# DeltaNet and a low-rank mixer on one core: where the second unit of each batch's first pass is multiplied by its inverse

## The chip, the cores and the metric

The kernel runs on one core of a Trainium2 chip. The metric is device time in microseconds, lower is better. Three runs of the kernel before gave 590.03, 590.49 and 590.49 us, a median of 590.49.

## The reference

Two blocks follow each other. The first is a DeltaNet layer over 4 batches, 8 heads, 768 steps and 48 channels, a recurrence with a 48 x 48 state per head; the second is a mixer over the 768 tokens of 384 channels, with a rank-32 product over the tokens and a two-layer perceptron over the channels.

```python
k_n = k / (np.linalg.norm(k, axis=-1, keepdims=True) + 1e-06)
for t in range(S):
    y[:, :, t] = einsum('bhd,bhde->bhe', q[:, :, t], state)
    v_old = einsum('bhde,bhd->bhe', state, k_n[:, :, t])
    state += beta[:, :, t] * einsum('bhd,bhe->bhde', k_n[:, :, t], v[:, :, t] - v_old)
x = y.transpose(0, 2, 1, 3).reshape(B, S, H * D)          # (4, 768, 384)
u = x + (x.transpose(0, 2, 1) @ U @ V).transpose(0, 2, 1)  # U (768, 32), V (32, 768)
out = u + np.maximum(u @ w_ch1, 0.0) @ w_ch2               # 384 -> 1536 -> 384
```

The arrays of the mixer arrive in float64 and are turned into float32 on the chip.

## The kernel before

The recurrence is done in chunks of 64 steps. A batch has twelve chunks (c = 0 to 11) and is split into two units of six chunks each: unit n = 2 * batch + half, so units 0 and 1 are the first batch. For a unit the kernel forms, for all eight heads and six chunks together:

- the products of the keys with themselves and with the queries (`grams`: transposes L668 or L405 on PE, copies L682 on ACT, products L704, then L714 and L725 on ACT, L717 and L736 on DVE);
- the norms and the scales with beta (`norms`: the square root L611 on ACT, then L614 to L619 on DVE);
- the inverse Z of a triangular 64 x 64 matrix per chunk and head (`blocks`): a transpose L781, a substitution on DVE step by step (L790 and L796), a transpose back L803, and joins of the 32 x 32 blocks on PE and ACT (L847 to L926).

`recur` then walks over the chunks. With s the state, a chunk needs z = Z (v - K s) and gives s + K z (L1135 on PE, L1147 on DVE, tile `s`) and the output (L972 and L986 on PE, copied to X by L956 on ACT). There are two ways to z, chosen by the set `LATE` of unit numbers. For a unit that is not in LATE, `prepare` forms Z K (L1011 on PE, L1030 on ACT) and Z v (L1022, L1035) ahead, in two halves of three chunks, and a chunk takes one product (L1107) and one subtraction (L1120, tile `z`). For a unit in LATE the chunk takes the product with the plain keys (L1066), subtracts (L1078, tile `w`), multiplies by Z (L1090) and copies (L1099, tile `z`):

```python
nc.vector.tensor_tensor(out=w..., in0=vn[:, cu]..., in1=p_b, op=ALU.subtract)   # L1078
for j, par, g in heads:
    nc.tensor.matmul(states(p_z)[half(g ^ par), par, j], pg[half(g), par, cu, j],
                     w[half(g), 2 * par + j], start=True, stop=True)             # L1090
z = zs[c] = small.tile([128, 4, D], FP32, name="z", bufs=3)
nc.scalar.copy(z.rearrange("p (r j) d -> p r (j d)", r=2), p_z)                  # L1099
```

At the same time the mixer's weights are read in fourteen slices and turned from float64 bits into float32 by five DVE steps (L1244, L1250, L1256, L1262, L1272) and one ACT step (L1229) each; the slice `u_sb` is the first. Two buffers, `X` and `wide`, and for two slices `hs`, take the raw slices in turn, and DVE frees them with L1262.

When all twelve chunks of a batch stand in X, the mixer takes it in three groups of 256 tokens. `front` forms tt = U^T x once per batch (L1469 on PE, L1476 on DVE), the rank-32 product (L1486) and its sum into X (L1495 on DVE), and turns the group around (L1514, or L405 where it is done in quadrants of the PE array; the copy to `ut` is L1517 on ACT). `wide` does the two channel layers (L1580, L393 in quadrants, and L1545; then L1695 and L1620). Some groups of the later batches use sums of blocks that save products (L1430, L1412, L1607).

Nothing is ordered by a scheduler while it runs. Each part of the kernel is a Python generator, and a table `ORDER` (L147) holds, for every engine and for the DMA queues of SP, a written list of part numbers that says whose next instruction comes. `PARTED` (L264) names the parts that work in 64 x 64 quadrants of the PE array. Part 1 loads half of the first unit's keys from ACT's queue and then issues a warm-up square root on a constant tile (L559); part 8 is `norms` of unit 0, 9 and 19 are the key products of units 0 and 1, 11 and 21 their `blocks`, 2 the first half of beta's transposes (L579, L587), 4 the recurrence of batch 0, 78 the weights, 81 the first `front`. A change of the table that a square root or another function needs is put into the program as an instruction of its own.

Of the kernel before, what the change touches and what calls it, by code (L numbers as in the profile page):

```python
# [26 lines left out]
def kernel(  # L27
# [100 lines left out]
    def advance(i, value, at):  # L128
# [20 lines left out]
        9.0 9.1 9.0.0.0 9.1.0.0 2*2 19.0 19.1 3 19.0.0.0 3 19.1.0.0 10.0 10.1 10.0.0.0 20.0 11.4 10.1.0.0  # L149
        11.4 11.2*2 11.4*2 11.2*2 20.1 11.4*4 20.0.0.0 11.2*4 20.1.0.0 4.1 4.0*2 4.1 21.2*2 4 4.4 21.2 4  # L150
        21.2 4.5 4 21.4*2 21.2 4 4.5 4.6 4*2 21.2 4.6 21.2*2 4.7 4*2 4.8 4.7 4 21.4 4.9 4 21.4 4 4.9 4.8
        4.2*2 21.4*2 4 4.10 21.4*2 4*2 4.10 4.11 4*2 4.11 4.3 32.0 31.0 4.3 31.1 4.12 4 31.0.0.0 31.1.0.0 4
        4.12 32.1 4.13 4*2 4.13 4.14 4 4.15 4 4.14 4.15 79 32.0.0.0 81 32.1.0.0 81*2 40.0 82 98.0*2 39.0
        39.1 82 98.1 40.1 39.1.0.0 39.0.0.0 98.1 98.2 33.2*2 98.2 98.3*2 98.4 33.4*2 33.2 98.4 33.2 98.5
        33.4*2 33.2*2 98.5 98.7 83 33.2 33.4 33.2 33.4 98.7 33.4*2 98.8 5 5.0 5 40.1.0.0 5 98.8 5.1 5 98.9 5
        98.9 5 5.1 98.9 5 98.9 5.2 5 98.10 5 5.2 5.3 5 99.0 5 99.0 5 5.3 5.4 5 99.0 5 99.0 5.5 5 99.1*2 5
        5.4 99.1*2 5.5 40.0.0.0 5 83 99.2*2 99.3*2 99.4 48.0 99.4 41.2*2 47.0 99.7 47.1 47.0.0.0 47.1.0.0
        41.4*2 99.5*2 48.1 41.2 41.4*2 41.2 99.7 99.8 48.1.0.0 5 99.8 5.6 5 48.0.0.0 5 99.9 5 99.9 5.7 5*2
        99.9 5 5.6 99.9 5.8 5.7 5 99.10 5*2 100.0 5.9 5 100.0 5.8 5 100.0 5 100.0 5.9 5 5.10 5 100.1 5.11 5
        5.10 100.1 5 5.11 100.1*2 84 100.2*2 100.3*2 100.4*2 100.5 100.7 100.5 49.2*2 55.0.0.0 84 55.1.0.0  # L160
        100.7 100.8 49.2 49.4*2 49.2 100.8 84 100.9*2 6 85 100.9 6 100.9 56.0.0.0 56.1.0.0 6 100.10 49.4*2
        6.0 6 101.0*2 85 6.1 6 101.1*2 6 101.1 6 101.1 6.2 6 101.2*2 6.1 6 101.2*2 6 6.3 6.2 101.3 6 101.3 6
        6.4 6.3 6 101.4 6 101.4 6.5 6 101.4 6 101.4 6.4 6 6.5 101.5*2 101.7*2 57.2*2 57.4*2 86 57.4*2 57.2*2
        101.8*2 101.9*2 63.0.0.0 101.10 6 101.10 6 63.1.0.0 102.0*2 86 6.6 6 102.1*2 64.0.0.0 6 6.6 102.2 6
        102.2 6.7 6 102.2*2 6 6.7 102.3 6 102.3 6.8 6 102.3 6 102.3 6.9 6 102.4 6 102.4 6.8 6 102.4 6 102.4
        6.10 6 102.5*2 6.9 6.11 102.5 6 102.5 6.10 6 102.7 6.11 102.7 87 102.7*2 64.1.0.0 87 102.8*2 102.9*2
        102.10 71.0.0.0 103.0*2 71.1.0.0 103.1*2 103.2*2 103.3*2 65.4*2 65.2*2 103.4*2 72.1.0.0 65.2*2
        65.4*2 103.5*2 87 103.7 7 72.0.0.0 7 103.7 7 7.0 103.8*2 7.1 7 103.8*2 7 88 7 103.9*2 7 7.1 7.2 7
        103.10 7 7.2 104.0 7 104.0 7.3 7 104.0*2 7 7.3 7.4 104.1 7 104.1 7 104.1*2 7.5 7 7.4 104.2 7 104.2
        88 104.3*2 7 7.5 73.4*2 73.2*2 104.4*2 104.5 73.4*2 73.2*2 104.5 7 104.7 7 7.6 7 104.7 7 7.7 104.8  # L170
        7.6 7 104.8 7 104.8 7 104.8 7 7.7 7.8 7 104.9 7 7.8 7.9 7 104.9 7 89 7 104.10 7 7.9 7.10 7 7.11 7
        104.10 7 7.10 7.11 79 93.2 93.1 79 89 93.4 93.2 93.1 93.3 93.2 93.3 93.4 93.1 93.5 93.1 93.2 93.1
        94.2 94.3 93.1 90 94.3 94.4 94.2 90 94.1 105.3*2 94.1 94.2 90 94.1 94.5 94.1 94.4 94.2 105.4*2 105.5
        94.1 105.5 94.1 91 105.6 95.2 95.1 91 95.4 106.3 95.2 95.3 95.1 106.3 95.1 95.3 95.4 95.1 95.2
        106.4*2 95.5 95.1 106.5 95.2 96.3 95.1 106.5 96.1 106.6 92 96.4 96.2 96.1 92 96.2 96.4 96.1 96.2
        96.3 96.2 96.1 107.3*2 107.4*2 96.1 96.5 107.5*2 96.1 107.6 97.1 97.4 97.2 97.1 97.3 97.2 97.1
        108.3*2 97.1 97.3 97.2 97.5 108.4*2 97.1 97.2 108.5 97.1 108.5 108.6 97.4 109.3*2 109.4*2 109.5*2
        109.6
# [3 lines left out]
        78.14 3 10.0.0.0 11.2 18 78.15 21 78.15 10.1.0.0 10.0.0.0 21 18 21 11.4*2 10.1.0.0 11.4 21*3 11.2*3  # L182
        8 21 78.15 21*7 20.0.0.0*2 21*2 20.1.0.0 21 20.1.0.0 78.15*2 21.2 21.4 18 78.16 4 78.16*4 4 78.17*2
        4 21.2*3 78.17*3 4 78.18*2 4 78.18*3 4 78.19*2 4 78.19 4 78.19 4 78.19 78.20*2 4 78.20 21.4 4
        78.20*2 21.4 78.21 21.4 78.21*4 4 78.22*2 4 78.22*2 4 78.22 4 78.23*2 4 78.23*3 78.24*5 4 78.25*2
        31.0.0.0*2 31.1.0.0*2 4 33 4 30 4 78.25 4 33*2 4 78.25*2 33*2 78.26 32.0.0.0 78.26 81 33 78.26 81
        32.1.0.0*2 78.26 33 78.26 33 82 33*2 32.0.0.0 30 33*8 33.4 33.2 78.26.1*3 39.0.0.0 78.27 98.2.1*3
        39.1.0.0 78.26.1 39.0.0.0 30 78.27*4 39.1.0.0 33.2*3 33.4*2 78.27.1 33.4 41 98.5.1*2 78.27.1*2
        98.7.0 98.5.1 78.27.1 38 83 41 98.6 5 98.7.1 41*3 38 98.8.0 5 98.8.1 41*3 5 41 5 41*2 40.1.0.0
        98.9.0 41 98.9.1 5 40.1.0.0 41 98.10.0 5 41*2 5 41 5 41*2 5 41 5 41*15 41.2 5 99.2.1 40.0.0.0 99.2.1  # L190
        38 40.0.0.0 99.2.1 99.7.0 41.4 47.0.0.0*2 47.1.0.0*2 49 99.5.1*3 46 49*2 46 49*2 99.7.1 99.8.0 99.6
        5 48.1.0.0*2 99.8.1 49*2 48.0.0.0 5 48.0.0.0 49 5 49*2 5 49*2 5 99.9.0 49*2 99.9.1 49 99.10.0 5 49 5
        49*2 5 49 5 49*2 5 49 5 49*9 46 49*2 84 49 100.2.1*2 49.2 49.4 55.1.0 55.0.0 100.5.1*2 100.2.1
        100.5.1 100.7.0 84 55.1.0.0 55.0.0.0 55.1.0.0 100.7.1 55.0.0.0 100.6 57 100.8.0 54 100.8.1 56.0.0
        57*4 56.1.0 6 85 100.9.0 56.0.0.0 56.1.0.0 56.0.0.0 6 57 56.1.0.0 100.9.1 100.10.0 57*7 6 57 6 57*2
        6 57*2 6 57*3 101.2.1 57 6 57 6 57*2 6 57 6 57*5 6 54 57*3 57.2 101.2.1 101.7.0 57.4 101.2.1
        101.5.1*3 101.7.1 54 86 101.6 101.8.0 101.8.1 63.0.0 64.0.0 101.9.0 101.9.1 63.1.0 63.0.0.0 6
        63.0.0.0 101.10.1 101.10.0 64.1.0 63.1.0.0*2 65 62 65*2 6 65 64.0.0.0 62 6 64.0.0.0 65*2 6 65*2 6
        65*3 6 65 6 102.2.1 65 6 65 6 65*3 6 102.2.1*2 65 6 65 102.5.1*2 65 62 87 65 102.5.1 102.7.0 65*3
        102.7.1 65 102.8.0 65 102.6 102.8.1 87 65 102.9.0 65 71.0.0 65 102.9.1 102.10.0 64.1.0.0*2 71.1.0  # L200
        65*4 71.1.0.0 65 71.0.0.0 65.4 71.0.0.0 71.1.0.0 65.2 73 72.1.0 72.0.0 70 73*2 72.1.0.0 103.2.1 73
# [287 lines left out]
    LATE = set(range(2,8))  # L489
# [452 lines left out]
    def recur(b):  # L942
# [834 lines left out]
```

## Time and profile before

| what | value |
|---|---|
| median of three runs | 590.49 us |
| the profiled execution | 589.15 us |
| its span | 587.4 us |
| PE busy | 545.3 us (93%) |
| DVE busy | 456.2 us (78%) |
| ACT busy | 227.3 us (39%) |
| GpSimd busy | 118.1 us (20%) |

The span is the time from the first to the last event on the core; the time of the execution has 1.75 us more around it. PE is the matrix engine, DVE the vector engine, ACT the scalar engine, POOL is GpSimd, SP issues DMAs. Busy time does not tell what bounds: it has to be read by stretch. In the slices of the span each digit is the busy share of a fortieth (14.7 us) in tenths. A timeline row has start, duration, engine, line, operation, tiles, shapes and count, and in brackets the idle time before it and what released it. On PE one instruction of the program in float32 shows as two or more records.

### The profile page before, as it was taken

To read this page: it belongs to the slowest core of one execution; us is meant where nothing else is said; L and a number is where in the kernel's file an instruction comes from. 1 tells how busy PE (TensorE), PEld (TensorE's weight loads), DVE (VectorE), ACT (ScalarE), POOL (GpSimd) and SP (SyncE) were. 2 spreads that over 40 slices of the span, in tenths; PEclk is the share of its full clock that TensorE was granted. 3 is DMA by queue.
4 is the path that set the end of the run, shared out by engine and by line. 5 is a ranking of instruction groups with operands and counts; after the bars stand their busy time and mean duration, and the time that the engine had idled before them with its cause. 6 is when DMAs were issued, how large, how long until landed. Compare 5 with 4: busy or idle time off the path is not lost.

```text
span 587.4 us, 25542 instructions
## 1 busy us (share of the span) xinstructions
PE 545.3 (93%) x11460; PEld 491.1 (84%) x11460; DVE 456.2 (78%) x1086; ACT 227.3 (39%) x483; POOL 118.1 (20%) x205
## 2 busy tenths in 40 slices
PE   5697778799999999999999999999999999999997
PEld 4586677588888987997897798988889999999997
DVE  6898999999899898899878888888547574555552
ACT  4447476544433623344344305324423422131220
POOL 8132050311205304340252253301000000000000
PEclk9576666799999999999999999999999999999999
DMA  9634676652104314223212433200000000000013
GB/s 157 85 76 128 192 188 166 134 91 63 29 4 83 68 22 83 74 53 63 48 30 61 80 75 71 60 29 3 2 5 1 2 1 1 1 2 1 1 42 119
DMA packets 79213, 35.17 MB, mean 60 GB/s; under 512 B 65600, under 2 KB 76992, under 8 KB 79104
## 3 DMA queue, kind: packets, MB, share of 16 engines
q1 hardware_dynamic: 71200, 24.10, 18.9%
q0 software_dynamic: 6304, 9.15, 7.2%
q8 instruction: 90, 1.47, 1.0%
q10 hardware_dynamic: 1600, 0.30, 0.3%
q14 instruction: 19, 0.16, 0.1%
HBM read 28.80 MB, written 4.72 MB: 57 GB/s over the span
## 4 chain that ended last, share of the span: by engine, by line
PE 79%; DVE 7%; ACT 5%; DMA 4%; issue 3%; SPq 1%; POOL 1%; DVEq 0%; ACTq 0%; POOLq 0%
PE P L1695 24%; PE P L1580 12%; PE P L1430 12%; PE P L393 10%; PE P L704 3%; DMA wide<-in_moe_w_ch_dram 2%; PE P L668 2%; PE P L1066 2%; PE P L1090 1%; PE P L972 1%; PE P L1486 1%; PE P L986 1%; PE P L1135 1%; PE P L1514 1%; PE P L861 1%
## 5 line engine op out<-in xcount | busy, mean ns | idle before, releaser
L1695 PE MATMUL P<-w_sb,hs 128*128 128x192 f32 x480 | 84.2, 329 | 0.1
L1580 PE MATMUL P<-ut,w_sb 128*128 128x256 f32 x348 | 81.8, 386 | 0.1
L1695 PEld LDWEIGHTS P<-w_sb,hs 128*128 128x128 f32 x480 | 77.7, 190 | 1.3 <-issue 0.3
L1580 PEld LDWEIGHTS P<-ut,w_sb 128*128 128x128 f32 x348 | 64.1, 190 | 9.4 <-issue 0.6
L796 DVE TENSOR_TENSOR xt<-xt,prod 128x112 f32<-128x112 f32 (+21 forms) x200 | 64.6, 323 | 6.9
L790 DVE TENSOR_TENSOR prod<-gs,xt 128x112 f32<-128x112 f32 (+21 forms) x200 | 63.7, 319 | 3.9
L1620 DVE TENSOR_TENSOR X<-X,P 128x192 f32<-128x192 f32 x86 | 29.6, 349 | 36.1 <-PE P L1695 34.2
L1545 ACT ACTIVATE hs<-P 128x512 f32<-128x512 f32 x42 | 24.8, 597 | 62.1 <-PE P L1580 51.0
L393 PE MATMUL P<-ut,w_sb 64*64 64x256 f32 x624 | 43.0, 384 | 1.2 <-ACT hs L1545 0.9
L956 ACT COPY X<-P 64x192 f32<-64x192 f32 x96 | 30.0, 312 | 28.8 <-PE P L986 27.2
L704 PE MATMUL P<-slot 48*64 48x64 f32 x1536 | 33.5, 245 | 1.9 <-ACT slot L682 1.6
L704 PEld LDWEIGHTS P<-slot 48*64 48x64 f32 x1536 | 30.0, 157 | 6.1 <-ACT slot L682 2.5
L933 POOL MEMSET slot<- 32x384 f32 x32 | 13.4, 420 | 102.6 <-PE P L890 40.4
L1412 DVE TENSOR_TENSOR hs<-hs,P 128x512 f32<-128x512 f32 x30 | 20.1, 684 | 17.5 <-PE P L1430 9.2
L1695 PE MATMUL P<-w_sb,S 128*128 128x192 f32 x192 | 33.7, 330 | 0.0
L926 ACT COPY slot<-zz 32x384 f32<-32x384 f32 x64 | 32.3, 508 | 1.0
L1099 ACT COPY z<-P 128x192 f32<-128x192 f32 x36 | 11.5, 319 | 53.3 <-PE P L1090 46.4
L1695 PEld LDWEIGHTS P<-w_sb,S 128*128 128x128 f32 x192 | 31.1, 190 | 0.6 <-DVE xt L796 0.3
L548 POOL DMA_DIRECT2D slot<-in_k_dram x44 | 28.7, 657 | 12.3 <-PE P L1135 10.6
L668 PE MATMUL P<-ident,slot 128*128 128x128 f32 x108 | 20.0, 343 | 11.3 <-DMA slot<-in_k_dram 5.7
L1430 PE MATMUL P<-slot 128*128 128x128 f32 x240 | 29.7, 276 | 0.0
L1695 PE MATMUL P<-w_sb,slot 128*128 128x192 f32 x168 | 29.1, 327 | 0.0
(171 smaller groups left out, 1140.9 us busy)
## 6 DMA issues: line engine op xcount, KB each, us to landing
out_dram<-X SPq DMA_DIRECT2D x22, 192.0 KB, 2.0
X<-in_moe_w_ch_dram SPq DMA_DIRECT2D x10, 384.0 KB, 4.4
wide<-in_moe_w_ch_dram SPq DMA_DIRECT2D x10, 384.0 KB, 4.4
slot<-in_k_dram SPq DMA_DIRECT2D x48, 72.0 KB, 3.7
slot<-in_k_dram POOLq DMA_DIRECT2D x44, 72.0 KB, 3.1
slot<-in_v_dram SPq DMA_DIRECT2D x32, 72.0 KB, 3.7
slot<-in_v_dram POOLq DMA_DIRECT2D x32, 72.0 KB, 3.2
hs<-in_moe_w_ch_dram SPq DMA_DIRECT2D x4, 384.0 KB, 5.7
```

The lines of the kernel that those rows point to most:

```text
L393: nc.tensor.matmul(to[half(g)], w[half(r), half(g)], x[half(r)], start=start, stop=stop, skip_group_check=True,)
L548: queue.dma_start(out=t[half(1 - g if name == "z" else g), :, to, 0:D], in_=src[b, 4 * g + s, hf * UC * L : (hf + 1) * UC * L, :].rearrang ...
L668: nc.tensor.transpose(p_t[:, c // 3, c % 3], t[:, c, 2 * j : 2 * j + 2].rearrange("p s d -> p (s d)"), ident,)
L704: nc.tensor.matmul(p_g[half(g ^ (par * i)), par, c], kq[rows, c, j, 0, half(g)], kq[rows, c, j, i, half(g)], start=True, stop=True,)
L790: nc.vector.tensor_tensor(out=prod, in0=gb[:, :, j : j + 1, j + 1 :].to_broadcast([128, split, m, w]), in1=xb[:, :, 0:m, j : j + 1].to_bro ...
L796: nc.vector.tensor_tensor(out=xb[:, :, 0:m, j + 1 :], in0=xb[:, :, 0:m, j + 1 :], in1=prod, op=ALU.subtract,)
L926: nc.scalar.copy(pg[quarter(i), :, at, :, a : a + BK], cut(zc, h)[quarter(i)].rearrange("p r (c j) t -> p r c j t", j=2),)
L956: nc.scalar.copy(x[half(c % 2), c // 2, 4 * D * g : 4 * D * (g + 1)].rearrange("p (j r d) -> p r j d", r=2, d=D), states(p_y)[half(g)],)
L1430: nc.tensor.matmul(bank[:, q], w_block(w)[:, q // 2, 128 * (q % 2) : 128 * (q % 2) + 128], token(b, i, t), start=c == 0 and q == 0, stop=True,
L1580: nc.tensor.matmul(p_f[:, x], w(x, t), ut[:, t], start=(t == 0), stop=(t == KT - 1))
L1620: nc.vector.tensor_tensor(out=to, in0=to, in1=p, op=ALU.add)
L1695: nc.tensor.matmul(to, of[0], of[1], start=of[2], stop=of[3], skip_group_check=True)
```

## The change

`LATE` takes in unit 1, so that `prepare` runs for unit 0 alone, and chunks 6 to 11 of the first batch go the way with L1066, L1078, L1090 and L1099. The lists of all five engines are written anew, and PARTED loses 81, 102.7, 103.8 and 104.10 and gains 87. Part numbers below 4 and from 5 on mean the same in both; the children of part 4 are renumbered, since two of them are gone.

```diff
-    LATE = set(range(2,8))
+    LATE = set(range(1,8))
```

The beginning of ACT's list (1 after the first four is the warm-up square root, 8 the square root of unit 0's norms, 9.x.x.x the steps after unit 0's products, 19.0.0 the copy L682 for unit 1):

```diff
-        1*4 9.0.0 1 9.1.0 9.0.0.0 9.1.0.0 78.14.0 2*2 9.0.0.0*2 8 19.0.0 9.0.0.0 9.1.0.0*3 19.0.0.0 19.1.0
+        1*4 9.0.0 9.1.0 9.0.0.0 9.1.0.0*2 2*2 9.1.0.0 19.0.0 8 9.1.0.0 9.0.0.0*3 19.1.0 1 3 19.0.0.0
```

The beginning of DVE's and of PE's list, and of POOL's queue:

```diff
-        9.0.0 9.1.0 78.14*3 9.0.0.0*2 9.1.0.0*2 78.14 11 2 8 11*12 8 11 19.0.0.0*2 11*4 19.1.0.0*2 11.4 21
+        9.0.0 9.1.0 9.0.0.0*2 9.1.0.0*2 11 2 78.14 8 11*14 19.0.0.0*2 3 19.1.0.0 11*3 19.1.0.0 78.14*2 11.2
...
-        9.0 9.1 9.0.0.0 9.1.0.0 2*2 19.0 19.1 3 19.0.0.0 3 19.1.0.0 10.0 10.1 10.0.0.0 20.0 11.4 10.1.0.0
+        9.0 9.1 9.0.0.0 9.1.0.0 19.0 2*2 19.0.0.0 3 19.1 19.1.0.0 3 10.0 10.1 20.0 10.0.0.0 10.1.0.0 11.2*4
...
-        11.0 13 23 78.0 2*3 17 23 25 23 13 23 25 13*2 25 29 25 21.0 15*2 29 17 15*2 11.3 11.1 11.3 11.1 27*4
+        13 2 23*2 13 2*2 11.0 29*2 78.0 23*2 25 13*2 25 15 25 21.0 15 25 17 15*2 11.1 27 11.3 27 11.1 17 27
```

DVE's list where the first `front` stands (81; 4 are the steps of the recurrence, 78.25 and 78.26 two slices of weights, 33 the substitution of unit 2):

```diff
-        31.0.0.0*2 31.1.0.0*2 4 33 4 30 4 78.25 4 33*2 4 78.25*2 33*2 78.26 32.0.0.0 78.26 81 33 78.26 81
+        4 78.22 4 78.23*3 4 78.23 4 78.23 78.24*5 78.25 4 31.0.0.0*2 4 31.1.0.0*2 33 4 78.25 4 30*2 4 78.25
+        4 78.25*2 33*5 81 33*2 81 32.0.0.0*2 33*3 32.1.0.0 33 78.26*3 33 32.1.0.0 33 82 33*2 78.26 33*2
```

In the built program the instruction that loads ACT's table for square roots stands ahead of L559 before, and ahead of L611 after. On PE the first `front` is followed by these instructions (the counts are the program's; 668 on slot_88 are the transposes of unit 3):

```
before: L1469 x12, L704 x24, L1486 x8, L405 (X) x24, L405 (slot_88) x24, L1486 x8, L1580 x6, L668 x12, L1514 x6
after:  L1469 x12, L1486 x8, L704 x48, L1514 x6, L1580 x9, L1486 x8, L405 (slot_88) x24, L668 x18, L1514 x6
```

(The lines of the kernel after are three lower from L150 on; the numbers here are those of the kernel before.)

More of the change, by code (lines that the diff above doesn't have):

```diff
@@ L154 @@
[L154 to L163, printed above, removed]
@@ L262 @@
+        76*4 103.9.1 103.10.0 107.5.1 107.6.0 108.6.0 105.5.1 104.9.1 105.6.0 104.10.0 108.5.1 109.5.0
+        109.3.1 106.5.1 106.6.0 109.5.1 109.6.0
         """,
```

184 lines of the change are left out of this document (92 added, 92 removed), and 4 rows, old and new, of the table pe.

## Prediction

> **What bounds the kernel now.** I read the slices of the span first, then busy times in two windows (cut where the first wide layer's matmuls begin), then who waited for whom on DVE, then the timeline of ACT, DVE and PE around the places that the change touches.
>
> ```profile
> PE   5697778799999999999999999999999999999997
> DVE  6898999999899898899878888888547574555552
> ```
>
> In the first eight slices (some 118 us) DVE is the fuller engine, and from the ninth on it is PE. The windows say it in numbers:
>
> ```profile
> core 0: us, PE busy (x) PEld busy (x) DVE busy (x) ACT busy (x) POOL busy (x), PEclk, DMA share, GB/s
> 0.00:121.50 121.50, 89.43 (x2763) 79.36 (x2763) 108.48 (x250) 68.15 (x129) 39.28 (x71) 0.71 0.67 142
> 121.50:587.40 465.90, 455.90 (x8702) 411.78 (x8698) 347.77 (x837) 159.13 (x355) 78.84 (x134) 1.00 0.17 39
> ```
>
> Up to 121.50 us PE works 89 of 121 us at a granted clock of 0.71 and DVE 108; after it PE works 455.90 of 465.90 us at full clock. So the second stretch cannot shrink by more than 10 us, and it starts when the first token mixing (tt at L1476, the sum at L1495) is through DVE. What DVE waits for until then:
>
> ```profile
> DVE slot L736 <- ACT slot L914: 0.9, 1, 0.9
> DVE power L1244 <- DMA X<-in_moe_w_ch_dram: 0.6, 1, 0.6
> DVE power L1244 <- DMA wide<-in_moe_w_ch_dram: 0.6, 2, 0.4
> DVE norm L614 <- ACT norm L611: 0.5, 1, 0.5
> DVE s L1147 <- PE P L1135: 0.4, 1, 0.4
> DVE z L1120 <- PE P L1107: 0.3, 1, 0.3
> ```
>
> Columns: total us, times, longest. From 15 to 121 us that is 3.7 us with two smaller rows. DVE runs its list almost without a hole: whatever makes it later before 118 us makes the end later, unless these 3.7 us give way. Of them only 0.7 us are the recurrence's.
>
> **The change part by part** (line numbers are those of the kernel before).
>
> *The product with the inverse.* Removed for unit 1: two halves of prepare. The profile has a half of L1011 as 48 records in 1.5 us (94.20 to 95.7) and of L1022 in 1.3 us (98.41), so 2 x 2.8 = 5.6 us of PE, and on ACT 2 x (0.80 + 0.65) = 2.9 us. Added for chunks 6 to 11: six L1090 (16 records; its neighbours L986 and L1107 take 0.41 to 0.68 us in this stage), 2.5 to 4 us of PE, and six ACT copies L1099 of 0.32, 1.9 us. DVE's six L1120 (347 ns) become six L1078 (350 ns): nothing. PE and ACT have over 25 us to spare each before 121.50, so these totals cost and bring nothing by themselves; if DVE did not cover them, PE would gain 1.6 to 3.1 us.
>
> *The chain of chunks 6 to 11.* From w to s it now runs DVE 0.35, PE 0.45, ACT 0.32, PE 0.45 and some 0.3 of handovers: 1.9 us. The changed program's DVE list holds, from w to the next s, work (each instruction at its row's mean) of 3.4, 2.4, 5.8, 3.1 and 1.7 us: only the last is short, by 0.2. From s to w the path is 1.1 us (s 0.35, product 0.45 to 0.68, handover), or 1.66 as from 109.23 to 110.89, where another product stood ahead; the list holds 1.3, 1.3, 1.3, 1.2, 0.9, 1.3. So the stalls are 0.4 us at the least and 2.9 at the most. Behind a waiting w or s on DVE stand the weight conversions (L1244 to L1272), and for these PE's first wide layer waits. At tt the list since w of chunk 11 holds 4.75 us; the path took 5.36 from z to tt (110.89 to 116.25) with 0.8 of L704 in between, which now stands behind, and z comes 0.9 later: 5.4, a stall of 0.65. Against this go the kernel's own 0.9 of such stalls (0.4, 0.3 and a row of 0.2), and the DMA wait of 0.6, as that conversion now stands behind the first sum at L1495. Bounds -0.5 and +2.0; I take +0.6, nearer the low end, because the stalls that a row shows are 0.2 to 0.4 each.
>
> *The table of sqrt.* This is the part of the new queues that I price highest. Before, the warm-up sqrt (L559) stands second on ACT:
>
> ```profile
> 6.06 0.48 ACT L677 COPY slot<-P 128x384 f32<-128x384 f32 x1 [1.13 <-PE P L668]
> 6.56 1.28 ACT L559 ACT_TABLE_LOAD   x1
> 7.85 0.20 ACT L559 ACTIVATE warm<-warm 128x1 f32<-128x1 f32 x1
> ...
> 15.01 0.26 ACT L611 ACTIVATE norm<-gs 128x32 f32<-128x32 f32 x1 [0.37 <-DVE gs L781]
> ```
>
> The load of 1.28 us lies where ACT waits for PE (1.68 us before L714 at 10.27), and the first real sqrt starts 0.03 us after its input. In the changed ACT queue the warm-up comes after that sqrt, and the built program has the table load directly ahead of L611, behind L682 too. From the rows: L714 ends at 10.85 and 11.80, and the four L717 (some 0.37 each) no longer stand behind u_sb's conversion, so the last two end, and L725 can start, at about 12.6; then L725 0.80, L587 0.30, L729 0.62, L682 0.80, load 1.28, sqrt 0.26 end near 16.75. DVE's norm (L614), at 15.30 now, comes near 16.8: +1.5. Behind it on DVE waits the whole substitution of unit 0, then all else. Bounds: 0 if the 3.7 us of waits swallow it; +4.3 if the transposes L405 of unit 1, now ahead of beta's L579 on PE, wait for their load until 13.82 as they do now. Its load is issued by 5.6 us in the new POOL queue and landed some 5.3 us after its issue before, so near 11, when L704 ends on PE (11.14): I keep 1.5.
>
> [...]
>
> *DVE's list from that norm to tt.* At its rows' means it is 101.3 us in both programs (it took 100.95 us): u_sb's steps moved behind the norm are made up by the last weight's three steps moved behind tt. Zero.
>
> *The first front.* Now PE covers the wait for ACT's copy (L1517):
>
> ```profile
> 118.83 0.93 PE L405 MATMUL P<-ident,X 64*64 64x64 f32 x48 [1.31 <-DVE X L1495]
> 119.58 1.11 PE L405 MATMUL P<-ident,slot 64*64 64x64 f32 x48
> 120.68 0.88 PE L1486 MATMUL P<-tt,v_sb 64*64 64x192 f32 x16
> 121.49 2.86 PE L1580 MATMUL P<-ut,w_sb 128*128 128x256 f32 x12
> ```
>
> From tt (116.25) to L1580 it is 5.24 us. Changed, nothing stands between the transposes (L1514 in place of L405) and L1580: tt 0.44, L1486 0.82, sum 0.95, transposes 0.92, copy 0.90 with handovers make some 4.2 us, and the 2.0 us of L405 and L1486 come after. 4.2 + 2.0 - 5.24 = +0.9; bounds 0 and 2.
>
> *The rest.* From there the lists hold the same products; three fewer narrow and front steps in quadrants cost the same (48 quadrant records or 12 whole ones, both near 2 us); changes of tile shape go from 137 to 138, and one costs 0.2 us (twelve L1695 take 1.95 or 2.15 us in the chain). I take 0, with -3 and +4 as bounds: PE is idle for 10 us here, of which 3 could go, or 4 come to it.
>
> Sum: 1.5 + 0.6 + 0.9 = +3.0 us. The profiled execution took 589.15 us (span 587.4 and 1.75 around it); 592.15 by this sum. The median of the runs is 590.49, 1.34 above that execution, so the forecast is 593.5.
>
> **The rivals.**
>
> *The recurrence paces, and gets shorter (faster).* For: s of chunk 5 is at 80.43 and the product of chunk 6 starts at 85.33, released by ACT L1030 of prepare, 4.55 us after s was there; and 2.8 us of L1011 and L1022 stand in PE's queue from 94.20. If these set the stage, it changes by -4.55 - 2.8 + 6 x 1.0 = -1.35 us and the norm has slack: 589.1. Against: DVE worked on all through it (30.02 of the 32.25 us from 84.00 to 116.25) and took z of chunk 6 only at 88.51. It decides if DVE's holes after the norm stay under 2 us.
>
> *The recurrence paces, and gets longer.* Each chunk adds product, copy and handovers, about 1.0 us; six make +6 in place of the 0.6 above, with the 1.5 and 0.9: 599 at the most, 597 with the two stalls of prepare partly gone. It decides if DVE's work between w and s is under 1.9 us; that holds in one of five places.
>
> *Absorbed (the change shifts work but no time).* The 1.5 us is swallowed by DVE's 3.7 us of waits, and the front costs nothing: 590.5. Against: most of those waits follow DVE's own work and shift with it.
>
> *The dense stage pays.* New orders there bring +4: 597.5. I find no place for it.
>
> **How the numbers follow.** Forecast 0.45, recurrence longer 0.13, dense stage worse 0.13, absorbed 0.16, faster 0.13. The forecast's own range is 591.7 to 595.5. The range 589.3 to 597 leaves out most of the faster case below and part of the two slow ones above, together 0.2. A change under 0.2% (1.2 us) cannot be told from none here. Slower than 591.7: 0.45 + 0.13 + 0.13, 0.71; within: 0.16; faster: 0.13.
>
> **What would show it.** The table load ahead of L611 between 15 and 17 us and DVE's L614 near 16.8; tt near 118.4; L1580 first near 122.6 behind an idle PE; six L1099 before 118 us without DVE waits over 0.5 us; PE idle for about 10 us after its start. It would be wrong if L614 stays near 15.3, if tt is before 117, or if PE's idle time after the front changes by more than 3 us.

## The result: 6.3 us slower

| | before | after |
|---|---|---|
| median | 590.49 us | 596.81 us (596.02 to 602.23, four runs) |
| ratio of the runs | 1 | 1.0122, 95% interval 1.0096 to 1.0147 |
| profiled execution, its span | 589.15, 587.4 us | 596.14, 594.3 us |
| norm on DVE (L614, after: L611) | 15.30 us | 17.60 us |
| tt on DVE (L1476, L1473) | 116.25 us | 118.73 us |
| first wide product (L1580, L1577) | 121.49 us | 124.69 us |
| from there to the end of the span | 465.91 us | 469.61 us |

Measured again later, beside its variants, the changed kernel took 597.98 us against 590.76, ratio 1.0118 (1.0088 to 1.0147). The ratios are estimated from all runs in the usual state and not from the two medians, which would give 1.0107 here; one run of late_alone at 781.0 us and one of keep_warm_before at 599.67 us are not in that state and are left out below. Lines of the kernel after are three lower than those of the kernel before. Only unit 1, the second half of the first batch, changes its way; units 2 to 7 stood in LATE already.

The picture is the same as before: DVE is the fuller engine up to the first wide product, then PE to the end. What changed is seen only by stretches. The windows, cut at the first wide product (start and end, length; busy us of PE, PEld, which is the loading of PE's weights, DVE, ACT and POOL; granted clock; DMA's busy share; GB/s):

```profile
0.00:124.69 124.69, 93.10 (x2561) 82.33 (x2561) 108.08 (x253) 65.29 (x129) 42.84 (x76) 0.64 0.68 140
124.69:594.30 469.61, 458.37 (x8624) 413.92 (x8624) 348.12 (x833) 159.80 (x354) 76.22 (x129) 1.00 0.17 38
```

DVE does the same 108 us of work in the first stretch, which is 3.2 us longer; the clock there is 0.64 instead of 0.71. In the second PE is busy 2.47 us longer and idle 11.24 us in place of 10.00. The timeline of the changed kernel around norm (start, length, engine, line, operation, what ended the idle time):

```profile
8.05 1.51 PE L665 MATMUL P<-ident,slot 128*128 128x128 f32 x6 [1.38 <-DMA slot<-in_k_dram]
...
16.02 1.28 ACT L608 ACT_TABLE_LOAD   x1
17.31 0.26 ACT L608 ACTIVATE norm<-gs 128x32 f32<-128x32 f32 x1
17.60 0.18 DVE L611 TENSOR_SCALAR norm<-norm 128x32 f32<-128x32 f32 x1 [1.48 <-ACT norm L608]
```

Two things make norm 2.30 us late. The table load stands in front of it, as announced. But the transposes of the second half of k of unit 0 also start at 8.05, where they started at 7.20 after a wait of 0.53 us: their load landed 0.85 us later. The rest of the list up to tt took 101.13 us (17.60 to 118.73), and 100.95 before. What DVE waited for in that stretch for norm and in the recurrence (15 to 124.69 us; total, times, longest; the other rows are 0.9 us or less):

```profile
DVE norm L611 <- ACT norm L608: 1.5, 1, 1.5
DVE w L1075 <- PE P L1063: 0.7, 2, 0.4
DVE s L1144 <- PE P L1132: 0.5, 2, 0.3
```

The recurrence's own waits (w and s) are 1.2 us, none over 0.4. Then the first front:

```profile
118.73 0.36 DVE L1473 COPY tt<-P 128x192 f32<-128x192 f32 x1 [0.31 <-PE P L1466]
119.14 1.56 PE L1483 MATMUL P<-tt,v_sb 64*64 64x192 f32 x16 [0.51 <-DVE tt L1473]
120.48 2.52 PE L701 MATMUL P<-slot 48*64 48x64 f32 x96
122.93 0.87 PE L1511 MATMUL P<-ident,X 128*128 128x128 f32 x6
124.69 4.15 PE L1577 MATMUL P<-ut,w_sb 128*128 128x256 f32 x18 [0.89 <-ACT ut L1514]
```

PE waits 0.89 us for ut, as forecast. But L1483 takes 1.56 us (0.82 before), and the 96 records of L701 (48 products) 2.52, for PE had only half its clock here. The windows of 4 us from 112 us on, first of the kernel before, then of the kernel after (the clock is the third number from the end):

```profile
112.00:116.00 4.00, 3.98 (x88) 2.78 (x92) 3.23 (x9) 1.99 (x4) 4.00 (x7) 0.50 1.08 240
116.00:120.00 4.00, 2.69 (x124) 2.26 (x120) 3.97 (x9) 0.54 (x2) 3.37 (x6) 0.95 1.31 170
120.00:124.00 4.00, 4.00 (x74) 3.29 (x67) 3.86 (x10) 1.43 (x2) 0.00 (x0) 1.00 0.66 90
```

```profile
112.00:116.00 4.00, 2.48 (x68) 2.19 (x72) 3.52 (x6) 1.68 (x5) 3.70 (x6) 0.54 1.08 212
116.00:120.00 4.00, 3.49 (x52) 2.10 (x56) 3.31 (x14) 0.98 (x4) 3.82 (x8) 0.50 1.32 167
120.00:124.00 4.00, 3.80 (x114) 3.35 (x106) 2.97 (x7) 0.16 (x1) 3.08 (x5) 0.68 1.26 168
```

Both kernels have a stretch of half clock in front of the dense stage (before from 109.6 to 116.4 us, after from 112.3 to 122.6); after, it lies later and covers the front. Last, there is work that the kernel before did ahead of its first wide product and the changed one does behind it. PE's groups of that kind from the first wide product to the end, before and then after (busy us, mean ns):

```profile
L1486 PE MATMUL P<-tt,v_sb 64*64 64x192 f32 x164 | 9.0, 330 | 0.0
L1514 PE MATMUL P<-ident,X 128*128 128x128 f32 x60 | 8.2, 274 | 0.3 <-ACT X L956 0.3
L405 PE MATMUL P<-ident,X 64*64 64x64 f32 x48 | 0.9, 222 | 0.0
```

```profile
L1483 PE MATMUL P<-tt,v_sb 64*64 64x192 f32 x176 | 9.6, 332 | 0.0
L1511 PE MATMUL P<-ident,X 128*128 128x128 f32 x54 | 7.5, 275 | 0.2 <-ACT slot L679 0.2
L402 PE MATMUL P<-ident,X 64*64 64x64 f32 x96 | 1.9, 220 | 0.0
L402 PE MATMUL P<-ident,slot 64*64 64x64 f32 x48 | 0.9, 218 | 0.0
```

They are 18.1 us before and 19.9 after: 1.8 us more is left to do. So in the two traces the 6.9 us of span are: norm 2.30, list to tt 0.18, tt to the first wide product 5.96 - 5.24 = 0.72, left-over work 1.8, the rest of the dense stage 3.70 - 1.8 = 1.9. (The dense stage is the part from the first wide product to the end, in which PE is busy almost throughout.)

In that rest PE waits longer for the recurrences of the later batches. Two of the rows of PE's waits from the first wide product on, before and then after:

```profile
PE P L1135 <- ACT z L1099: 0.9, 3, 0.5
PE P L1066 <- DVE s L1147: 0.6, 1, 0.6
```

```profile
PE P L1132 <- ACT z L1096: 1.5, 5, 0.5
PE P L1063 <- DVE s L1144: 1.3, 4, 0.5
```

All rows for z, s and w together are 4.3 us before and 6.0 after; early_norm and front_cover below show the same 6.0.

One pair of traces does not fix these parts to a tenth. front_bare, below, has the program of the kernel before up to the first front, and shows norm at 15.14 and tt at 118.84, so that the stage between them took 103.70 us where the trace of before has 100.95. That trace is the quickest of the four whose lists are the old ones between norm and tt (the other two: 102.42 in late_table, 103.20 in both_alone).

### The profile page after: what moved, and what is told of

It reads as the page before. It is cut to its first block, busy times and chain, and to the rows that moved or that the text cites. A ratio compares the mean times of both kernels' runs of the same rounds, so it can differ in the third digit from the quotient of the medians.

```text
span 594.3 us, 24968 instructions
## 1 busy us (share of the span) xinstructions
PE 551.5 (93%) x11184; PEld 496.2 (83%) x11184; DVE 456.2 (77%) x1085; ACT 225.1 (38%) x483; POOL 119.1 (20%) x205
## 4 chain that ended last, share of the span: by engine, by line
PE 79%; DVE 11%; ACT 5%; issue 2%; DMA 2%; ACTq 0%; DVEq 0%; SPq 0%
PE P L1692 25%; PE P L1577 13%; PE P L1427 11%; PE P L390 8%; PE P L701 4%; PE P L1063 2%; PE P L1087 2%; PE P L1483 2%; PE P L858 2%; PE P L983 2%; PE P L1132 1%; DVE prod L787 1%; PE P L969 1%; DVE xt L793 1%; PE P L844 1%
## 5 line engine op out<-in xcount | busy, mean ns | idle before, releaser
L1692 PE MATMUL P<-w_sb,hs 128*128 128x192 f32 x516 | 90.4, 330 | 0.0
L1692 PEld LDWEIGHTS P<-w_sb,hs 128*128 128x128 f32 x516 | 83.3, 190 | 1.7 <-issue 0.6
L1577 PE MATMUL P<-ut,w_sb 128*128 128x256 f32 x348 | 81.0, 385 | 1.4 <-ACT ut L1514 0.9
L1577 PEld LDWEIGHTS P<-ut,w_sb 128*128 128x128 f32 x348 | 64.3, 190 | 10.8 <-ACT ut L1514 1.1
L1692 PE MATMUL P<-w_sb,S 128*128 128x192 f32 x216 | 38.0, 329 | 0.0
L701 PE MATMUL P<-slot 48*64 48x64 f32 x1536 | 32.9, 242 | 4.5 <-ACT slot L679 2.8
L701 PEld LDWEIGHTS P<-slot 48*64 48x64 f32 x1536 | 30.1, 155 | 7.9 <-ACT slot L679 4.4
L1692 PEld LDWEIGHTS P<-w_sb,S 128*128 128x128 f32 x216 | 34.9, 190 | 0.3
L1096 ACT COPY z<-P 128x192 f32<-128x192 f32 x42 | 13.4, 318 | 51.4 <-PE P L1087 51.1
L1427 PEld LDWEIGHTS P<-slot 128*128 128x128 f32 x240 | 28.6, 192 | 0.3
```

Source lines behind the costliest of these rows:

```text
L701: nc.tensor.matmul(p_g[half(g ^ (par * i)), par, c], kq[rows, c, j, 0, half(g)], kq[rows, c, j, i, half(g)], start=True, stop=True,)
L1427: nc.tensor.matmul(bank[:, q], w_block(w)[:, q // 2, 128 * (q % 2) : 128 * (q % 2) + 128], token(b, i, t), start=c == 0 and q == 0, stop=True,
L1577: nc.tensor.matmul(p_f[:, x], w(x, t), ut[:, t], start=(t == 0), stop=(t == KT - 1))
L1692: nc.tensor.matmul(to, of[0], of[1], start=of[2], stop=of[3], skip_group_check=True)
```

## The experiments

Five theories. Theory 1: norm is late, the first front uncovered, and each goes to the end one for one. Theory 2: the longer chain of chunks 6 to 11 costs by itself. Theory 3: the half clock in front of the dense stage costs. Theory 4: the new order of the dense stage costs. Theory 5: it is the place of the moved products in the queues that costs. All times are medians; the ratio is to the kernel before on the same chip.

| run | base | us | ratio (95%) | norm | first wide product | from there to the end |
|---|---|---|---|---|---|---|
| late_alone | before | 596.67 | 1.0077 (1.0049-1.0105) | 16.36 | 127.66 | 466.94 |
| late_tuned | before | 599.94 | 1.0124 (1.0091-1.0157) | 15.93 | 129.34 | 471.86 |
| late_table | before | 593.16 | 1.0011 (0.9993-1.0028) | 16.66 | 124.32 | 468.58 |
| front_bare | before | 593.18 | 1.0018 (0.9998-1.0037) | 15.14 | 123.50 | 470.10 |
| both_alone | before | 592.95 | 1.0023 (1.0006-1.0039) | 16.45 | 124.22 | 467.38 |
| keep_warm_before | before | 594.44 | 1.0026 (0.9998-1.0055) | | | |
| after_again | after | 597.98 | 1.0118 (1.0088-1.0147) | 17.53 | 125.61 | 471.49 |
| warm_back | after | 596.64 | 1.0068 (1.0043-1.0094) | 15.98 | 124.51 | 472.09 |
| dma_head | after | 596.39 | 1.0064 (1.0040-1.0087) | 16.73 | 122.95 | 469.75 |
| early_norm | after | 594.94 | 1.0040 (1.0022-1.0058) | 15.59 | 122.13 | 470.07 |
| early_cover | after | 594.19 | 1.0054 (1.0034-1.0074) | 15.59 | 123.30 | 469.20 |
| front_cover | after | 596.96 | 1.0092 (1.0064-1.0119) | 17.60 | 125.39 | 469.51 |
| keep_warm | after | 597.71 | 1.0082 (1.0053-1.0111) | 18.36 | 124.36 | 470.04 |
| early_warm | after | 596.38 | 1.0077 (1.0053-1.0102) | 16.73 | 122.55 | 471.05 |
| after_unlate | after | 609.02 | 1.0252 (1.0202-1.0301) | 18.09 | 127.91 | 479.29 |
| graft_only | after | 609.73 | 1.0319 (1.0278-1.0360) | 17.84 | 124.58 | 479.92 |
| graft_early | after | 607.91 | 1.0275 (1.0243-1.0307) | 15.67 | 122.58 | 485.22 |
| dense_back | after | 598.33 | 1.0099 (1.0070-1.0129) | 15.52 | 123.10 | 471.50 |

The last three columns are those of one profiled execution each (keep_warm_before's isn't used). They scatter: the same program shows 124.69 and 469.61 in one and 125.61 and 471.49 in the other (after_again). Chips differ too (the kernel before has medians of 590.76 to 592.76 us on them), so variants are compared by their ratios.

> The changed kernel unaltered, as the measure for the three others on the same chip. Both theories: 1.2% over the kernel before (1.010 to 1.015), as first measured.

### Norm

The warm-up square root back in its place (**warm_back**; ACT's list), and the memset of xt back at the head of POOL's list (**dma_head**); both in **early_norm**:

```diff
-        1*4 9.0.0 9.1.0 9.0.0.0 9.1.0.0*2 2*2 9.1.0.0 19.0.0 8 9.1.0.0 9.0.0.0*3 19.1.0 1 3 19.0.0.0
+        1*4 9.0.0 1 9.1.0 9.0.0.0 9.1.0.0*2 2*2 9.1.0.0 19.0.0 8 9.1.0.0 9.0.0.0*3 19.1.0 3 19.0.0.0
...
-        13 2 23*2 13 2*2 11.0 29*2 78.0 23*2 25 13*2 25 15 25 21.0 15 25 17 15*2 11.1 27 11.3 27 11.1 17 27
+        11.0 13 2 23*2 13 2*2 29*2 78.0 23*2 25 13*2 25 15 25 21.0 15 25 17 15*2 11.1 27 11.3 27 11.1 17 27
```

> The changed kernel with the warm-up square root back in its old place on ACT, so that the table load lies at about 6.5 us. If the load on the way to the norm costs: DVE's first norm at 16.2 to 16.4 in place of 17.60, tt and the end 1.2 to 1.5 us earlier, 595.0 to 595.7. If the end follows the windows of PE's granted clock and not DVE's list: no change, or a whole window (3.4 us) at once, 593.4.

> The changed kernel with the first memset of xt (L772) back at the head of POOL's list, as before; nothing else. In the changed kernel POOL's first loads of q, beta and k start at 2.81 us in place of 3.73, and the second half of k of unit 0 lands 0.85 us later. Theory 1 (POOL's earlier loads take the DMA engines from that half): the second group of L665 starts at 7.2 in place of 8.05, norm starts at 16.4 to 16.5 in place of 17.3, and the time falls by up to 0.85 to about 596. Rival: the order of SP's own loads is what delays it, the second L665 stays at 8.05 and the time at 596.8.

> The changed kernel with both: the memset of xt at the head of POOL's list, and the warm-up square root of L556 back behind ACT's first copy of k, so that the table is loaded at 6.5 us. Theory 1 in full: norm at 15.3 as in the kernel before, and since DVE's list from norm to tt measured the same in both kernels (101.1 and 100.95 us), tt at 116.4 and the time near 594.5, with 2 to 2.5 us of late start gone. Theory 3: norm at 15.3, but the gain is lost in TensorE's half clock before 120 us as in the run with the warm-up alone, the first L1577 at 124 or later and the time 596 or more.

Norm came at 15.98, 16.73 and 15.59 us: the table load is worth 1.62 us of its 2.30, the place of one memset 0.87, both 2.01. The second is seen in no wait for POOL: POOL only issues its loads 0.9 us earlier (the first at 2.81 us after, 3.73 before), and the load of k that PE waits for lands later. That they compete for the DMA engines is my guess; no run shows it. The twenty traces agree with the effect: the second group of k's transposes starts between 7.88 and 8.81 us in all seven with the memset moved back, and no later than 7.5 in eleven of the thirteen with it at the head. In the other two, late_table and late_alone, it starts at 8.2, so there is a second cause for a late k that no run here isolates. ACT's timeline in early_norm:

```profile
6.77 1.28 ACT L556 ACT_TABLE_LOAD   x1
15.05 0.28 ACT L608 ACTIVATE norm<-gs 128x32 f32<-128x32 f32 x1
```

In time each of the two gives back 0.5 to 0.6%, and both 0.8% (1.0120, the mean of the changed kernel's two ratios, against 1.0040); the interval of early_norm doesn't touch those of the changed kernel. That is the largest single part, and theory 1 holds for it in kind: a late norm costs time. One for one it isn't shown. By the ratios the two edits give back 4.7 us (some 3.2 to 6.3, with the intervals put together), more than the 2.0 us by which norm moved, but on different chips; early_cover, measured beside after_again on one chip, gives back 3.8 us (some 1.7 to 5.9), the cover included. And in warm_back's trace the gain was gone by tt: norm at 15.98, tt at 119.55, against 17.60 and 118.73.

**late_table** is the converse in the kernel before: only the warm-up behind the square root.

```diff
-        1*4 9.0.0 1 9.1.0 9.0.0.0 9.1.0.0 78.14.0 2*2 9.0.0.0*2 8 19.0.0 9.0.0.0 9.1.0.0*3 19.0.0.0 19.1.0
+        1*4 9.0.0 9.1.0 9.0.0.0 9.1.0.0 78.14.0 2*2 9.0.0.0*2 8 19.0.0 9.0.0.0 9.1.0.0 1 9.1.0.0*2 19.0.0.0
```

> The kernel before, with only the warm-up square root of ACT moved behind the square root of norm, so that the table is loaded in front of norm, as in the changed kernel. Nothing else changes. Theory 1 (norm's lateness passes to the end one for one): the table load stands at 15.0 us, norm on DVE at 16.6 in place of 15.30, and the time is 1.3 us above the kernel before (0.5 to 2 with the noise). Rival: DVE's list has slack before the dense stage and hides it; time unchanged within 0.5 us.

Norm moved as expected, to 16.66 (here k was late as well; both_alone, below, has the same edit with k in time, and norm at 16.45). The ratio makes it 0.7 us slower, with an interval of -0.4 to 1.7: that agrees with 1.3, and isn't told from nothing.

### The first front

**front_cover**: transposes of unit 3 (part 40.0, which are its queries; the expectations call them k3 or the transposes of k) and the second L1483 back ahead of the first L1577 in the changed kernel. **early_cover**: early_norm, and only the second L1483 (82) ahead. The diff is early_cover's; front_cover moves 40.0 ahead of 82 as well.

```diff
-        4.13 4 4.12 4 4.13 79 81*2 32.0.0.0 32.1.0.0 81 98.0*2 98.1 82 40.0 40.1 39.0 39.1 82 39.0.0.0
+        4.13 4 4.12 4 4.13 79 81*2 32.0.0.0 32.1.0.0 81 82 98.0*2 98.1 40.0 40.1 39.0 39.1 82 39.0.0.0
```

> The changed kernel with the transposes of unit 3 (L405) and the second L1486 put back between the first front's transposes and the first wide product on PE. If the uncovered wait costs 0.9 us of idle PE: 595.6 to 596.2. If the half clock there costs more (these steps run at half clock now or later at full clock): no gain, 596.5 to 597.5.

> The changed kernel with norm early (warm-up square root and memset of xt back in place, as in the run before) and with the second L1483 moved ahead of the first L1577, where it fills the 0.9 us in which TensorE waits for ACT's copy of ut. Theory 1 (each late or uncovered piece adds to the end one for one): 2.3 + 0.9 us less than the changed kernel, 0.4 to 0.6% under it. Rival: the cover brings nothing, as when it was moved together with the transposes of k that wait for a load, and the time stays 2.3 us under the changed kernel.

front_cover failed for a reason of its own: in its trace the load for these transposes came late, and PE waited for it.

```profile
123.90 0.85 PE L402 MATMUL P<-ident,slot 64*64 64x64 f32 x41 [1.49 <-DMA slot<-in_q_dram]
```

So these transposes could not cover the front in the new order; the second L1483 could. early_cover took 594.19 us, 3.8 less than the changed kernel on the same chip, and within 0.15% of early_norm's ratio: what it gains is norm's; the cover itself isn't told from nothing.

**front_bare** and **both_alone** take the cover away in the kernel before, the second with the late table as well:

```diff
-        4.12 32.1 4.13 4*2 4.13 4.14 4 4.15 4 4.14 4.15 79 32.0.0.0 81 32.1.0.0 81*2 40.0 82 98.0*2 39.0
+        4.12 32.1 4.13 4*2 4.13 4.14 4 4.15 4 4.14 4.15 79 32.0.0.0 81 32.1.0.0 81*2 98.0*2 82 40.0 39.0
```

> The kernel before, with the transposes of k3 (L405) and the second L1486 moved from in front of the first L1580 to behind its first twelve products, as in the changed kernel; nothing else. Theory 1: TensorE waits some 0.9 us for ACT's copy of ut, the first L1580 stands 1.0 to 1.1 us earlier (two groups of 2.0 us out, a wait of 0.9 in), and the time rises by 0.9 us (0.5 to 2.5). Rival: the two groups fill later gaps of the dense stage, and the time is unchanged.

> The kernel before with both: table load in front of norm, and the first front without cover. If the terms add: 0.9 (measured for the table alone) + 0.9, 1.8 us above the kernel before, ratio 1.003. If both are late in one place and hide each other: ratio 1.001 to 1.002. If the kernel is more sensitive than its single terms, as the changed one seems to be: 1.005 or more.

PE's timeline in both_alone shows the uncovered wait, 0.92 us (the second L1486 and unit 3's transposes come behind these products):

```profile
124.22 2.86 PE L1580 MATMUL P<-ut,w_sb 128*128 128x256 f32 x12 [0.92 <-ACT ut L1517]
```

The bare front alone costs 1.1 us (-0.1 to 2.2), both together 1.4 us (0.4 to 2.3). That is the effect of the two largest terms of the forecast in a kernel that is otherwise the old one. They were forecast at 1.5 and 0.9, 2.4 together.

### The clock

**keep_warm** adds products that nothing reads, so that PE does not idle (early_warm the same on top of early_cover, keep_warm_before in the kernel before). `hot` is called once behind each of the two output products of chunks 8 to 11, and for two products each behind those of tt and of the first rank-32 product: twelve in all, 24 records in the trace, and not the 20 that the expectations name.

```diff
+    def hot(x, n):
+        for _ in range(n):
+            nc.tensor.matmul(P[:, BANK["pair"][x], 384:512], ident, ident, start=True, stop=True, skip_group_check=True)
```

> The changed kernel, and besides it 20 products of the 128x128 identity with itself into columns of P that nothing reads: one behind each of the two output products of chunks 8 to 11 in sequence 0, two behind the transposed mix of L1466, two behind the products of L1483. They add nothing that is read; they only keep TensorE from idling between 104 and 120 us. Theory 3 (the half-clock stretch of 10.2 us in front of the dense stage, a result of the sparse last chunks, is what the changed kernel pays beyond the forecast): the granted clock is 0.9 or more in 112 to 124 us instead of .54, .50 and .68, L1483 takes 0.8 us and the 96 matmuls of L701 1.6 us, the first L1577 stands near 123.0 in place of 124.7, and the time falls to about 594.5. Theory 1 (late norm and uncovered front, the clock no cause): the first L1577 stays at 124.7 or comes later by the added work of some 2 us, and the time is 597 or more.

> The kernel before with the same 20 added products. It has a half-clock stretch of 6.8 us (110 to 117 us) of its own. Theory 3: that stretch goes, and the time falls by 0.5 to 1.5 us below the kernel before. Theory 1: no gain, at most 2 us longer by the added work.

> The kernel with norm early and the second L1483 as cover, and the 20 added products of the identity as in the first run with them. Theory 3 (the half clock before the first front costs up to 2 us): the clock is 1.00 from 104 us on, L1483 0.82 to 0.88 us in place of 1.56, L701 1.7 in place of 2.4 to 2.8, the first L1577 1 us or more earlier than 122.1 to 123.3, the time 1 us or more under the same kernel without them (594.2, ratio 1.0054). Rival: the added work eats it, and the ratio is 1.005 or more.

In keep_warm and keep_warm_before the added products are marked as the start of a sum, in the bank where y, the chunk's output, is being summed, and their y is not the layer's; they stand here for their time alone. early_warm has start=False, and its y is the layer's. The windows of early_warm:

```profile
112.00:116.00 4.00, 3.52 (x93) 2.60 (x92) 3.31 (x7) 1.58 (x6) 3.52 (x7) 1.00 1.19 224
116.00:120.00 4.00, 2.98 (x77) 2.33 (x79) 3.17 (x12) 0.00 (x0) 3.74 (x7) 1.00 1.29 165
120.00:124.00 4.00, 3.92 (x89) 3.16 (x81) 3.79 (x12) 0.80 (x1) 2.35 (x4) 1.00 1.12 165
```

The half clock is gone; L1483 (here L1493) takes 0.88 us and L701 1.63. From tt to the first wide product it is 5.18 us, with the second L1483 ahead, in place of 5.83 in early_cover. The times do not agree. early_warm is not faster than early_cover (1.0077 against 1.0054, the intervals overlap), and keep_warm_before is not faster than the kernel before (1.0026, 0.9998 to 1.0055). But keep_warm, at 1.0082, lies 0.4% under the changed kernel's 1.0120, by the intervals 0.0 to 0.7%. Theory 3 holds for the length of the rows, 0.7 us at the front; as the cause of the loss two of three runs speak against it, and one allows some 2 us.

In the dense stage, where PE paces, half a clock does cost. In after_again the half stretch ran on past the first wide product (the slice of its page from 119.4 to 134.3 us has a clock of 6 tenths, that of the first trace from 118.9 to 133.7 us 8), and the same 18 records that took 4.15 us in the first trace took 5.78:

```profile
125.61 5.78 PE L1577 MATMUL P<-ut,w_sb 128*128 128x256 f32 x18 [0.89 <-ACT ut L1514]
```

These 1.63 us are most of the 1.88 by which the two traces of the changed kernel differ from there to the end. front_bare has the same (4.48 us for 12 records, 2.86 in before), and eight other traces have pieces of lower clock later in the stage (slices of some 15 us at 7 or 8 tenths on their pages), late_table (133.4 to 148.2 us) and warm_back (447.5 to 462.4 us) among them.

### The move by itself

**late_alone**: the lists of the kernel before, with unit 1 in LATE; the two halves of prepare taken out of PE's and ACT's lists, six p_z and six copies put in, each near the step that needs it. **late_tuned** has these at other places. **after_unlate** is the reverse: the changed lists with unit 1 prepared again.

```diff
-    LATE = set(range(2,8))
+    LATE = set(range(1,8))
...
-        4.2*2 21.4*2 4 4.10 21.4*2 4*2 4.10 4.11 4*2 4.11 4.3 32.0 31.0 4.3 31.1 4.12 4 31.0.0.0 31.1.0.0 4
+        21.4*2 4 4.8 21.4*2 4*3 4.8 4.9 4*3 4.9 4 32.0 31.0 31.1 4.10 4 31.0.0.0 31.1.0.0 4 4.10 32.1 4.11
```

> The kernel before with unit 1 in LATE and its own old lists of instructions: only prepare's steps of unit 1 taken out, and six products L1090 and six copies L1099 put in. If the new lists cost the time (norm of unit 0 late by 2.3 us, first front uncovered): 589.5 to 592. If the longer chain of chunks 6 to 11 itself costs it: 595 to 598, with tt 2 us or more later than the 116.25 of before.

> The move alone in the lists of the kernel before, as in the first run of that kind, but with the moved products, their copies and the sums around them put at other places in the queues of PE, ACT and DVE between chunk 6 and the first front. Theory 5 (the cost of the move is where it is put): fewer and shorter waits of DVE's s for TensorE (5.1 us in 5 waits in the first such run), the first front 1 to 2 us earlier, the ratio 1.003 to 1.006 in place of 1.0077. Theory 2 (a longer chain costs what it is long): no change, 1.0077 or more.

> The changed kernel's lists, but unit 1 prepared ahead as before (LATE from 2 on; the products L1090 and copies L1099 of chunks 6 to 11 out, prepare's steps back in). New lists as the cause: 595 to 598, as the changed kernel. The chain as the cause: 590 to 592.

DVE's waits in late_alone, 15 to 127 us:

```profile
DVE s L1146 <- PE P L1134: 5.1, 5, 1.2
```

Where the lists are not drawn for it, the longer chain does cost: 5.1 us in five waits for s (3.9 of it in four waits behind 80 us, where chunks 6 to 11 run), and 4.6 us of time (2.9 to 6.2). In the changed kernel the same chain waits 1.2 us, and its list from norm to tt is not longer: twelve traces with the new lists up to tt and unit 1 in LATE took 100.1 to 103.6 us for it, eleven of them under 102, where the four with the old lists and unit 1 prepared ahead took 101.0 to 103.7, late_alone 106.0 and late_tuned 106.8. late_tuned was no better (its s waits 5.4 us), so theory 5 has no support from it; after_unlate was 2.5% slower, with waits of its own at my places for prepare, and tells nothing of the move. Theory 2 holds for the old lists; for the changed kernel the traces don't bear it out.

### The dense stage

**graft_only** and **graft_early** (the second with norm early and the cover): from the first L1577 on the old order on PE, DVE and ACT and of the last stores. **dense_back**: the old order on all five queues. The edit is the tail of each list, and PARTED as before but without 81.

```diff
-        4.13 4 4.12 4 4.13 79 81*2 32.0.0.0 32.1.0.0 81 98.0*2 98.1 82 40.0 40.1 39.0 39.1 82 39.0.0.0
+        4.13 4 4.12 4 4.13 79 81*2 32.0.0.0 32.1.0.0 81 82 98.0*2 40.0 39.0 39.1 82 98.1 40.1 39.1.0.0 39.0.0.0
```

> The changed kernel up to its first L1577; from there on the queues of PE, DVE, ACT (and the last stores on SP) in the order of the kernel before, with its choice of split and whole products. Unit 1 stays inside the recurrence and norm stays late. Theory 4 (the new order of the dense stage itself costs: from the first L1577 to the end the traces read 465.9 us before and 469.5 to 470.1 in every kernel with the new lists): that stretch falls to 466 to 468 and the time by 2 to 3.5 us. Rival: the 3.7 us is only work of the first front left over (the second L1483, the transposes of k) and the recurrence of later units, which no order changes, and the time stays within 1 us of the changed kernel.

> All three: norm early, the second L1483 as cover, and the old order of the dense stage behind it; unit 1 still inside the recurrence. If theories 1 and 4 hold and add up: 2.3 + 0.9 + 2.5, 5 to 6 us less than the changed kernel and within 1.5 us of the kernel before, so that moving unit 1's products costs nothing by itself in these lists. If moving them costs the time of the move itself (theory 2): 2 us or more over the kernel before, whatever the lists.

> The changed kernel with norm early and the second L1483 as cover, and from the first L1577 on the order of the kernel before on all five queues, the loads too. Unit 1 is still inside the recurrence. Theory 4 (the new order of the dense stage costs 2 to 3.7 us): from the first L1577 to the end 466 to 467.5 us instead of 469.2 to 470.1, and the time within 1 us of the kernel before. Rival (left-over work of the first front, not the order): 469 to 470, and a ratio of 1.004 to 1.006 as in the two runs with norm early. A stretch of over 472 would say that the old order doesn't fit behind the new one, and tell nothing of either.

The two grafts don't answer: with the old order and the new load queues, DVE's scaling of v (L625) waits in graft_early for a load that the view names as one of q, and the stage is over 10 us longer in both:

```profile
DVE slot L625 <- DMA slot<-in_q_dram: 9.6, 1, 9.6
```

dense_back has all queues old, and its stretch to the end is 471.50 us, above what either theory expected and just under the limit set for a misfit; the time is 1.0099. So theory 4 isn't shown by its experiments. The stretch was 469.2 to 472.1 us in the nine traces with the new lists throughout and unit 1 in LATE. In those with the old lists and a covered front it was 465.91 (before), 466.94 (late_alone), 468.58 (late_table), and 471.86 in late_tuned. The traces whose pages show no piece of lower clock in this stretch compare best. With a bare front they are both_alone at 467.38 with the old lists, and the changed kernel's first trace, dma_head, early_norm and keep_warm at 469.61 to 470.07 with the new; front_bare, less its 1.6 us of half clock, is 468.5. That leans to a loss of 1 to 3 us in the new dense stage, and PE's longer waits for the later recurrences (6.0 us; 3.9 in both_alone) go with it; no edit that takes them away was run.

## Why the prediction was right in direction and wrong in size

It said 593.5 us, 3.0 above the median of before; the kernel took 596.8, just inside the range, with a loss of twice that size. The places were named rightly; what failed are the sizes of three terms. The first front was priced at +0.9 with 48 products of L704 (L701 after, 96 records) left out of its path and its rows taken at full clock, and the traces give 2.5. Norm was priced at +1.5 without the later load of k, and the traces give 2.3. And the rest of the dense stage was put at nothing because the lists hold the same products, and the traces give 1.9, part of it in waits that the new order makes longer.

| step of the forecast | forecast | in the two traces |
|---|---|---|
| the table of sqrt (norm) | +1.5 | +2.30 |
| DVE's list, chain of chunks 6 to 11 | +0.6 | +0.18 |
| the first front | +0.9 | 0.72 + 1.8 = +2.5 |
| the rest | 0 (-3 to +4) | +1.9 |
| sum | +3.0 | +6.9 |

**The table of sqrt**: right mechanism, mis-sized. The load stood where it was announced (15 to 17 us), took 1.28 us, and DVE waited 1.48; but norm came at 17.60, not near 16.8. The step weighed whether unit 1's load would come in time, and did not ask when the second half of k of unit 0 lands behind the new head of POOL's queue: 0.85 us later. dma_head shows it (0.87 back). In time the two edits that bring norm back were worth 4.7 us (3.2 to 6.3), more than even the 2.3; how the difference arises stays open. The load cost its own 1.28 us and little more: the copy before it ended at 16.00 and the load began at 16.02, and the load ended at 17.30 and the square root began at 17.31.

**The chain of chunks 6 to 11**: right, within the scatter of single traces. Waits of 1.2 us for w and s, none over 0.5, and 101.13 us from norm to tt. The +0.18 is against the quickest of the four old traces; against the other three the new lists are 1.3 to 2.6 us shorter here. That the chain stays hidden because the new lists put DVE work between w and s fits late_alone, where it doesn't.

**The first front**: right mechanism, mis-sized. The wait for ut is 0.89 us and the two groups came behind it. The step reckoned 4.2 us from tt to the first wide product with rows at full clock; it took 5.96, since L1483 took 1.56 in place of 0.82 and L701, which I had left out of the path, 2.52 with the transposes behind it. Other traces part the two: a bare front took 4.57 and 4.66 us with the old lists (both_alone, front_bare), and 5.19 with the new ones at full clock (keep_warm), so some 0.8 us of the 5.96 is the half clock's, and up to 1.7 in other traces (6.89 in after_again). Whether the half clock at the front matters in the time is open, and a bare front costs about 1.1 us in the old lists.

**The rest**: taken at nothing, at 1.9 us in the traces. PE's idle time grew by 1.2 us (11.24 against 10.00, within the 3 us announced); of its waits those for z, s and w of the later batches grew by 1.7, while some others shrank. The bound of +4 held it. That the lists hold the same products was right, and not enough: their order makes PE wait longer. What the waits are worth in time, and where the other 0.7 us went, stays open.

**The rivals.** The time is near those of two rivals, and neither is what happened. The recurrence did not pace: its list is as long as before. The dense stage paid, but less than a third of the loss. What was absorbed or faster did not occur.

By runs rather than traces: norm back in its place returns 0.6 to 0.8% of the 1.2%. The 0.4 to 0.5% that remain (2.4 to 3.2 us) are in the new lists with the front and the dense stage, and no part was shown to carry them alone. The terms of the forecast that are left without norm add up to 1.5. No version was found that beats the kernel before; the best of the changed ones, early_norm and early_cover, stay at 1.0040 and 1.0054.

## What to carry to other kernels

When the start of a queue is redrawn, follow the first item of the bounding engine's list back through every queue to its load, the queues that merely issue earlier among them: a memset moved back on POOL cost 0.87 us at norm, and PE's wait named only the load, not the queue that had moved. What an uncovered wait costs is the wait and the work left for later (here 0.89 and 1.8 us), at the clock that the stage will have, not at that of the row it is read from (L1483 took 1.56 us at half clock, 0.82 in the row of before). A move and the lists drawn around it are one change: the longer chain cost 4.6 us in the old lists and nothing measurable in the new ones, which lost as much elsewhere. And a stage read from one trace is good to some 2 us here: the same instructions took 100.95 and 103.70 us in two executions.

## What the runs showed of the hardware

The granted clock in front of the dense stage was either full or half: 1.00 or 0.50 in every window of 0.5 us from 100 to 129 us in the traces of before and after, but for the windows in which it changed. The half stretch was 6.8 us long before (109.6 to 116.4) and 10.2 us after (112.3 to 122.6). The half stretches ahead of it were 17.1, 17.1, 20.5 and 10.2 us long before and 13.7, 23.9 and 41.0 us after, and the shortest full ones between them 6.8 us before and 3.4 us after; all of these lengths are near multiples of 3.4 us. PE was shown busy 2.48 to 3.98 us of 4 in the windows at about half clock (0.50 and 0.54) and 2.98 to 3.92 in early_warm at full clock (1.00), so the busy share of the profile does not tell the two apart here. With the twelve added products of 128x128 the clock was 1.00 from 104 to 128 us in early_warm, and 9 tenths or more in each slice of keep_warm's page from 104 us on; without them it was 0.70 from 115 to 125 us in early_cover, and 0.54, 0.50 and 0.68 from 112 to 124 in the changed kernel. With them the first wide product came 1.1 to 2.1 us sooner after norm (106.0 and 105.8 us, against 107.1, 108.1 and 107.7 without), and only one of the two kernels was faster for it. In the dense stage a piece of half clock cost 1.6 us of wide products (5.78 us for the 18 records in after_again, 4.15 in the first trace).
